# Threshold attention and a Fourier mixer: bit operations of the weight conversion moved to PSUM, tau's transfer and the first transpose rearranged

## The chip, the cores and the metric

The kernel runs on one core of one Trainium2 chip, in one launch. The metric is the device time in microseconds (us). The core has a matrix engine (PE), a vector engine (DVE), a scalar engine (ACT), a general engine (POOL) and SP, which here only issues transfers. Each engine works through its own queue in program order, and engines wait for each other by semaphores. SBUF is the large on-chip memory, PSUM the small one into which PE writes.

## The reference

Inputs q, k, v are float32 of shape (8, 8, 576, 64); the two weight matrices, 512x2048 and 2048x512, come as float64.

```python
scores = scale * np.matmul(q, k.transpose(0, 1, 3, 2))
thresh = np.max(scores, axis=-1, keepdims=True) - tau
scores = np.where(scores >= thresh, scores, -1000000000.0)
attn = np.exp(scores - np.max(scores, axis=-1, keepdims=True))
attn = attn / (np.sum(attn, axis=-1, keepdims=True) + 1e-09)
x = np.matmul(attn, v)              # heads side by side: (8, 576, 512)
u = x + np.real(np.fft.fft(np.fft.fft(x, axis=1), axis=2))
un = (u - mean(u)) / np.sqrt(var(u) + 1e-06)
out = u + np.maximum(un @ w_ch1, 0.0) @ w_ch2
```

## The kernel before

**Attention.** Two heads make a pair, four pairs a batch. A pair is worked in five steps t = 0 to 4 of 128 query rows for each head (the fifth holds the two ends of 64). A step is: `scores` (PE, tile sc, L431 and L437), the row maximum `neg` (DVE, L455), the exponential `e` (ACT, L463) with the threshold `thr` (L467), the comparison with the threshold, which also sums the row (DVE, L471), and the reciprocal of the sum `den` (L485). One step later PE transposes e into the tiles pe and pw (`transposed_weights`, L534 to L552), ACT copies these into SBUF (ends and e_t, L540 to L556), and PE multiplies with v in the tile pv (`weighted_values`, L581); DVE or ACT takes the product out as x (L589). `prep_pair` transposes k and q of the next pair on DVE (kT, L402 and L403; qT, L405), `scale_q` multiplies q beforehand (L389 on ACT for the first pair, L391 on POOL for others), and `load_pair`, `load_v` issue the transfers, on SP's queue but for the first pair's k, which goes through ACT's.

**Conversion of the weights.** Each float64 weight matrix is read as pairs of 32-bit words in 16 chunks of 128x512 and rebuilt as float32. `convert` is a generator whose stages the steps call one by one: transfer of the raw words; then two bit operations on DVE, one cutting out the upper fraction bits (L297), one the exponent (L300); then on ACT fraction to float (L305) and exponent to a power of two (L308); then on DVE the lower word added (L312); then on POOL the product with the power (L317); at last the sign on ACT (L319) and its product on POOL (L320). Before the change the bits are written into the destination in SBUF, and the exponent into a spare region of SBUF, `power`, which ACT overwrites with the power of two.

One chunk of w_ch1 goes with each of the first 16 steps of batch 0 (`step`); the 16 of w_ch2 go with the steps of batch 1 by the table PLAN (`second_batch`), in which three steps, 5, 8 and 9, hold two chunks. POOL and DVE also take the column means out of w_ch1 (L377), with PE's help (pm, pr).

**Other work.** From batch 1 on, PE also does the Fourier mixing (py, pa) and the channel layers of the batch before (`channels` and `channels_in_quarters`: ph L814 and L918, po L840 and L1082, transposed rows pn L774), handed out between the steps by a budget. Where nothing else is due in batch 0, `busy` fills PE with matmuls on ones (pd, L112).

**Order and buffers.** In batches 0 and 1 the order of each engine is written out by hand: it is the order of the code. The kernel uses eight banks of PSUM: the two sc tiles hold two each, and all other tiles in PSUM (pd, pe, pw, pv, pm, pr, py, pa, pn, ph, po) share the pool with the tag "mm" of four banks. A tile of this pool starts when the last reader of the bank's former tile is done. Transfers wait by eight semaphores used in turn, so a transfer can wait for the one eight places before it.

Of the kernel before, what the change touches and what calls it, by code (L numbers as in the profile page):

```python
# [10 lines left out]
INT32 = mybir.dt.int32  # L11
UINT32 = mybir.dt.uint32
ALU = mybir.AluOpType
ACT = mybir.ActivationFunctionType
# [33 lines left out]
def kernel(  # L48
# [12 lines left out]
    nc = tc.nc  # L61
    B, H, S, D = q.shape
# [11 lines left out]
    WC = 512  # L74
# [10 lines left out]
    ps = ctx.enter_context(tc.tile_pool(name="ps", bufs=2, space=bass.MemoryType.PSUM))  # L85
# [38 lines left out]
    def load_pair(n, queue=nc.sync):  # L124
        b, p = n // NPAIR, PAIRS[n % NPAIR]
        hs = [2 * p + (j + p) % 2 for j in range(2)]


        raws = []
        for src, name, eng in ((q, "q_in", nc.sync), (k, "k_in", queue)):  # L130
            raw = sb.tile([128, S], FP32, tag=name, bufs=1, name=name)
            for j, h in enumerate(hs):
                for g in range(2):
                    p = 64 * j + 32 * g
                    eng.dma_start(
                        out=raw[p : p + 32, :].rearrange("p (r d) -> p r d", d=32),
                        in_=src[b, h, :, 32 * g : 32 * g + 32].rearrange(
                            "(r p) d -> p r d", p=32
                        ),
                    )  # L140
            raws.append(raw)
        loaded[n] = raws
# [10 lines left out]
            nc.sync.dma_start(out=vt[64 * j : 64 * j + 64, 8 + j, :], in_=v[b, h, 512:576, :])  # L153

    tau_t = const.tile([128, 1], FP32, name="tau_t")
    nc.scalar.dma_start(out=tau_t[:, :], in_=tau.partition_broadcast(128))
    load_pair(0, nc.scalar)


    ident = const.tile([128, 128], FP32, name="ident")  # L160
# [5 lines left out]
    for u in range(2):  # L166
# [14 lines left out]
        out=q_scale[:], in0=tau_t[:], scalar1=0.0, scalar2=SCALE, op0=ALU.is_ge, op1=ALU.mult  # L181
# [3 lines left out]
        out=below[:], in0=tau_t[:], scalar1=0.0, scalar2=-3.0e38, op0=ALU.is_lt, op1=ALU.mult  # L185
# [3 lines left out]
        out=tau_pos[:], in0=tau_t[:], scalar1=0.0, scalar2=-1.0, op0=ALU.max, op1=ALU.mult  # L189
# [87 lines left out]
    shift = const.tile([128, 1], FP32, name="shift")  # L277
    nc.vector.memset(shift[:], -float((1023 - 127) << 23))

    def convert(src, dst, raw, power):  # L280

        if src.dtype == FP32:
            nc.sync.dma_start(out=dst, in_=src)
            return
        nc.sync.dma_start(out=raw, in_=src.bitcast(INT32).rearrange("p (c n) -> p c n", c=2))
        pairs = raw.rearrange("p c (n two) -> p c n two", two=2)
        low, high = pairs[:, :, :, 0], pairs[:, :, :, 1]
        dst = dst.rearrange("p (c n) -> p c n", c=2)  # L290
        bits = dst.bitcast(INT32)
        power = power.rearrange("p (c n) -> p c n", c=2)
        sign = high.bitcast(FP32)

        yield

        nc.vector.tensor_scalar(  # L297
            out=bits, in0=high, scalar1=0xFFFFF, scalar2=None, op0=ALU.bitwise_and
        )
        nc.vector.tensor_scalar(  # L300
            out=power, in0=high, scalar1=20, scalar2=0x7FF,
            op0=ALU.logical_shift_right, op1=ALU.bitwise_and,
        )
        yield
        nc.scalar.activation(out=dst, in_=bits, func=ACT.Copy, bias=1.0, scale=2.0**-20)  # L305


        nc.scalar.activation(  # L308
            out=power, in_=power, func=ACT.Relu, bias=shift[:, :], scale=float(1 << 23)
        )  # L310
        yield
        nc.vector.scalar_tensor_tensor(  # L312
            out=dst, in0=low.bitcast(UINT32), scalar=2.0**-52, in1=dst,
            op0=ALU.mult, op1=ALU.add,
        )
        yield
        nc.gpsimd.tensor_tensor(out=dst, in0=dst, in1=power.bitcast(FP32), op=ALU.mult)  # L317
        yield
        nc.scalar.activation(out=sign, in_=high, func=ACT.Sign)  # L319
        nc.gpsimd.tensor_tensor(out=dst, in0=dst, in1=sign, op=ALU.mult)  # L320
# [74 lines left out]
    def prep_pair(n):  # L395

        q_raw, k_raw = loaded.pop(n)  # L400
        kT = sb.tile([128, D + S], FP32, tag="kT", name="kT")
        nc.vector.transpose(kT[:, D : D + S], k_raw[:, :])  # L402
        nc.vector.transpose(kT[64:128, 0:D], k_raw[64:128, 512:S])  # L403
        qT = sb.tile([128, S], FP32, tag="qT", bufs=1, name="qT")
        nc.vector.transpose(qT[:, :], q_raw[:, :])  # L405
        heads[n] = (qT, kT, v_in[n % 2])
        if n + 1 < B * NPAIR:
            load_pair(n + 1)
# [95 lines left out]
    def transposed_weights(i):  # L504
        for _ in weights_in_parts(i):
            pass
# [670 lines left out]
    def step(i):  # L1177

        n, t = divmod(i, NT)
        scores(i)  # L1180

        def stages(count):
            for _ in range(count if i - 1 in chunks else 0):
                next(chunks[i - 1], None)

        def next_stages():
            stages(2)

        def last_stage():
            stages(1)  # L1190
            chunks.pop(i - 1, None)

        if t == 1 and n > 0:
            softmax(i, lambda: weighted_values(n - 1, 1), next_stages, last_stage)
            load_v(n + 1)
        elif t == 3:
            softmax(i, lambda: weighted_values(n, 0), next_stages, last_stage)
        else:
            softmax(i, None, next_stages, last_stage)
        if t == 1 and n > 0:  # L1200
            pass
        elif later and later[0][0] <= i:
            later.pop(0)[1](i)
        else:
            busy(2 if i < NCHUNK else 1)
        if t == 2:
            scale_q(n + 1)
        if t == 3:
            prep_pair(n + 1)
        if t == 1:  # L1210
            prep_ends(n)
        if i in chunks:
            next(chunks[i])
        if i > 0:
            transposed_weights(i - 1)
        if i in chunks:
            next(chunks[i])
        while after and after[0][0] <= i:
            after.pop(0)[1]()
        if i > 0 and i + 3 < NCHUNK:  # L1220
            chunks[i + 3] = w1_chunk(i + 3)
        if t == 2 and n > 0:
            folds.append(fold_rows(n - 1))
        if folds and next(folds[0], True):
            folds.pop(0)
# [26 lines left out]
    chunks = {0: w1_chunk(0)}  # L1252
# [27 lines left out]
    chunks = {}  # L1280

    def advance(at):
        for run in chunks.get(at, ()):
            next(run, None)

    def transfers(first):
# [32 lines left out]
    def second_batch(i):  # L1319

        nonlocal budget
        n, t = divmod(i, NT)
        first = i - per_batch
        if first != 1:
            scores(i)
        if first == 0:

            transposed_weights(i - 1)
        softmax(
            i, None, lambda: (advance(first - 1), advance(first - 1)), lambda: advance(first - 1)  # L1330
        )
        chunks.pop(first - 1, None)
        transfers(first)
        fold_more()
        if first == 0:
            weighted_values(n - 1, 1)
            scores(i + 1)
            column_means(LAST)
            copy_mean(LAST)
            folds.append(fold_rows(n - 1))  # L1340
            while folds:
                fold_more()
            load_v(n + 1)
            start_batch(0)
            mix(3)
            mix(3)
        elif first == 1:
            mix(3)
            transposed_weights(i - 1)
            mix(2)  # L1350
            mirrored(LAST)
            for c, eng in ((1, nc.vector), (3, nc.vector), (0, nc.gpsimd), (2, nc.gpsimd)):
                less_mean(eng, LAST, c)
            advance(first)
            advance(first)
        elif first == 2:
            mix(2)
            transposed_weights(i - 1)
            mix(2)
            weighted_values(n, 0)  # L1360
            advance(first)
            advance(first)
        else:
            fill()
            transposed_weights(i - 1)
            advance(first)
            advance(first)
            fill()
            if t == 3:
                prep_pair(n + 1)  # L1370
            fill()
            if t == 2:
                weighted_values(n, 0)
            if t == 0:
                weighted_values(n - 1, 1)
                folds.append(fold_rows(n - 1))
                load_v(n + 1)
        if t == 1:
            prep_ends(n)
        if t == 2:  # L1380
            scale_q(n + 1)
        if first == 16:
            fold_halves(1)
        if first < 3:
            budget += 3 * per_slot
# [10 lines left out]
    for i in range(2 * per_batch, total + 1):  # L1396
# [4 lines left out]
        n, t = divmod(i, NT)  # L1401
# [79 lines left out]
```

## Time and profile before

| | |
|---|---|
| three timed runs | 1632.99, 1632.99, 1630.95 us |
| the profiled execution | 1633.26 us, span 1631.3 us, PE clock 0.994 of full speed |
| PE busy | 1583.8 us (97%) |
| weight loads into PE (PEld) | 1248.7 us (77%) |
| DVE busy | 1173.4 us (72%) |
| ACT busy | 817.8 us (50%) |
| POOL busy | 659.3 us (40%) |

Busy shares are means over stages that have different limits; a stage is read from the table of busy time by stretches. The chain of work that ended last is followed back from the end, and tells at each step what released it. In a line such as `w<-hs` the tile before the arrow is written, the one after it read, with buffer numbers left out; "x16" counts instructions, and a note in brackets says how long the engine was idle before it and for whom it waited. A line with DMA in it is a transfer, one with a q after the engine (SPq, ACTq) the issue of one.

### The profile page before, as it was taken

The page shows a single profiled execution, that of the slowest core. Times are in us where ns is not written, and L with a number is a line of the kernel's source. Part 1 is how long each engine was busy: PE and PEld are TensorE (multiplying, and loading weights), DVE is VectorE, ACT ScalarE, POOL GpSimd, SP SyncE. Part 2 cuts the span into 40 slices and gives each one's busy share as a digit, 9 for nine tenths or more (in the row PEclk, how much of TensorE's full clock was granted, in tenths as well). Part 3 has the DMA queues.
Part 4 walks back from the last instruction along what each step waited for, and adds up shares of the span by engine and source line. Part 5 has one row for each costly group of instructions (what it writes and reads, how often), then busy time and mean ns, then how long its engine had stood idle before and what let it go on. Part 6 is the DMA issues. An engine that isn't in the chain of part 4 may idle for free.

```text
span 1631.3 us, 27898 instructions
## 1 busy us (share of the span) xinstructions
PE 1583.8 (97%) x10346; PEld 1248.7 (77%) x10346; DVE 1173.4 (72%) x2518; ACT 817.8 (50%) x1738; POOL 659.3 (40%) x875
## 2 busy tenths in 40 slices
PE   8998999999999999999999999999999999999998
PEld 4555655577887888878888778877878788889998
DVE  7997886667758686857576868786787869664445
ACT  5765665544455454645445546454636455523111
POOL 6784673042421452244342244224352344124332
PEclk9999999999999999999999999999999999999999
DMA  6423222101110101110011010111111110000000
GB/s 162 123 56 113 74 75 57 40 17 22 20 38 17 34 9 43 23 29 16 21 23 36 17 34 11 41 23 35 17 27 32 22 29 2 14 7 7 14 14 14
DMA packets 203084, 57.41 MB, mean 35 GB/s; under 512 B 193827, under 2 KB 193829, under 8 KB 202950
## 3 DMA queue, kind: packets, MB, share of 16 engines
q1 hardware_dynamic: 200438, 55.34, 14.5%
q8 instruction: 82, 1.34, 0.4%
q10 hardware_dynamic: 2512, 0.30, 0.1%
q14 instruction: 52, 0.43, 0.1%
HBM read 46.02 MB, written 9.44 MB: 34 GB/s over the span
## 4 chain that ended last, share of the span: by engine, by line
PE 77%; DVE 14%; ACT 4%; POOL 2%; issue 2%; DMA 1%; SPq 1%; DVEq 0%; ACTq 0%; POOLq 0%
PE ph L918 24%; PE po L1082 20%; PE pv L581 9%; PE sc L431 7%; PE pw L552 6%; PE po L840 3%; DVE neg L455 2%; DVE e L471 2%; PE ph L814 2%; PE sc L437 1%; ACT e L463 1%; PE pn L774 1%; PE py L684 1%; PE pa L701 1%; DVE hs L1043 1%
## 5 line engine op out<-in xcount | busy, mean ns | idle before, releaser
L463 ACT ACTIVATE e<-sc,neg 128x576 f32<-128x576 f32 x288 | 212.5, 738 | 224.7 <-DVE neg L455 224.5
L455 DVE TENSOR_REDUCE neg<-sc 128x1 f32<-128x576 f32 x288 | 207.3, 748 | 161.6 <-PE sc L431 149.7
L471 DVE SCALAR_TENSOR_TENSOR e<-sc,thr,e 128x576 f32<-128x576 f32 x288 | 229.4, 812 | 42.2 <-ACT thr L467 40.4
L1082 PE MATMUL po<-w,hs 128*128 128x256 f32 x1024 | 246.2, 383 | 0.0
L1082 PEld LDWEIGHTS po<-w,hs 128*128 128x128 f32 x1024 | 186.1, 190 | 33.8 <-issue 12.8
L918 PE MATMUL ph<-u_t,w 128*128 128x128 f32 x1536 | 188.1, 277 | 0.0
L431 PE MATMUL sc<-kT,qT 64*128 64x288 f32 x1024 | 174.4, 433 | 12.6 <-DVE e L471 11.1
L918 PEld LDWEIGHTS ph<-u_t,w 128*128 128x128 f32 x1536 | 180.2, 193 | 5.0 <-issue 3.7
L552 PE MATMUL pw<-ident,e 128*128 128x128 f32 x1152 | 170.7, 275 | 7.8 <-ACT y_o L689 2.3
L554 ACT COPY e_t<-pw 128x512 f32<-128x512 f32 x256 | 148.8, 594 | 48.9 <-PE pw L552 48.2
L927 DVE TENSOR_TENSOR hs<-ph,hs 128x512 f32<-128x512 f32 x160 | 106.9, 685 | 70.7 <-PE ph L918 54.0
L431 PEld LDWEIGHTS sc<-kT,qT 64*128 64x128 f32 x1024 | 96.0, 187 | 78.1 <-issue 37.5
L552 PEld LDWEIGHTS pw<-ident,e 128*128 128x128 f32 x1152 | 134.9, 141 | 27.2 <-ACT y_o L689 4.2
L918 PE MATMUL ph<-t_u,s_w 128*128 128x128 f32 x1024 | 126.7, 277 | 2.1 <-POOL t_u L892 1.8
L918 PEld LDWEIGHTS ph<-t_u,s_w 128*128 128x128 f32 x1024 | 119.9, 192 | 7.4 <-issue 4.6
L1082 PE MATMUL po<-hs,s_tile 128*128 128x256 f32 x512 | 121.5, 381 | 0.0
L796 DVE SCALAR_TENSOR_TENSOR u<-po,rstd,u 128x256 f32<-128x256 f32 (+1 forms) x164 | 75.3, 483 | 63.9 <-PE po L1082 62.8
L492 ACT ACTIVATE e<-e,den 128x576 f32<-128x576 f32 x96 | 74.6, 777 | 76.5 <-DVE den L485 76.0
L1082 PEld LDWEIGHTS po<-hs,s_tile 128*128 128x128 f32 x512 | 94.0, 190 | 13.7 <-issue 2.5
L935 ACT ACTIVATE hs<-hs 128x512 f32<-128x512 f32 x112 | 69.2, 630 | 61.6 <-DVE hs L927 61.6
L614 POOL TENSOR_TENSOR half<-x 128x287 f32<-128x287 f32 x48 | 40.5, 865 | 119.5 <-ACT x L587 61.1
L1078 POOL TENSOR_TENSOR hs<-hs,s_tile 128x512 f32<-128x512 f32 x32 | 42.0, 1314 | 107.9 <-PE po L1082 85.0
(194 smaller groups left out, 2899.5 us busy)
## 6 DMA issues: line engine op xcount, KB each, us to landing
hs<-in_moe_w_ch_dram SPq DMA_DIRECT2D x23, 512.0 KB, 4.8
q_in<-in_q_dram SPq DMA_DIRECT2D x128, 72.0 KB, 2.5
out_dram<-u SPq DMA_DIRECT2D x36, 256.0 KB, 2.2
k_in<-in_k_dram SPq DMA_DIRECT2D x124, 72.0 KB, 2.5
v_in<-in_v_dram SPq DMA_DIRECT2D x64, 128.0 KB, 2.4
w<-in_moe_w_ch_dram SPq DMA_DIRECT2D x6, 512.0 KB, 3.6
stage<-in_moe_w_ch_dram SPq DMA_DIRECT2D x3, 512.0 KB, 3.6
v_in<-in_v_dram SPq DMA_DIRECT2D x64, 16.0 KB, 2.2
```

Of the source, the lines that this page charges most:

```text
L431: nc.tensor.matmul(sc[j][:, c, 0:HALF], qT[hp, 128 * t : 128 * t + 128], kT[hp, k0 + HALF * c : k0 + HALF * (c + 1)], start=True, stop=True,)
L455: nc.vector.tensor_reduce(out=neg[:, j : j + 1], in_=sc[j][:, :, 0:HALF], axis=AXIS_XY, op=ALU.max, negate=True,)
L463: nc.scalar.activation(out=ej, in_=sc[j][:, :, 0:HALF], func=ACT.Exp, bias=neg[:, j : j + 1], scale=1.0)
L471: nc.vector.scalar_tensor_tensor(out=ej, in0=sc[j][:, :, 0:HALF], scalar=thr[:, j : j + 1], in1=ej, op0=ALU.is_ge, op1=ALU.mult, accum_out ...
L492: nc.scalar.activation(out=e[:, S : 2 * S], in_=e[:, S : 2 * S], func=ACT.Copy, scale=den[:, 1:2])
L552: nc.tensor.transpose(pw[:, c, :], e[:, c0 : c0 + 128], ident[:, :])
L554: nc.scalar.copy(e_t[:, 4 * j : 4 * j + 4, qs], pw[:, :, :])
L581: nc.tensor.matmul(pv[64 * j : 64 * j + 64, 0:m], vt[:, 2 * c + j, :], e_t[:, 4 * j + c, 0:m] if c < 4 else ends[:, 0, 0:m], start=(c == 0 ...
L796: nc.vector.scalar_tensor_tensor(out=u, in0=product, scalar=self.rstd[:, t : t + 1], in1=u, op0=ALU.mult, op1=ALU.add,)
L918: nc.tensor.matmul(banks[name][:, 128 * q : 128 * q + 128], left[c][:, 512 * part + 128 * q : 512 * part + 128 * q + 128], right[c], start ...
L927: nc.vector.tensor_tensor(out=to, in0=bank, in1=to if other is None else other, op=ALU.add)
L1082: nc.tensor.matmul(bank[:, 0 : DM // 2], left[p], right[p], start=start and p == 0, stop=p == NK - 1, skip_group_check=True,)
```

## The change

The bits and the exponent go into two new PSUM tiles of the "mm" pool, and ACT reads them there; `power` receives only the power of two. Both stages (bit operations and ACT's reading) of a chunk now stand together, after the transposes of the step, in all three places that call them. At the start, tau's transfer (128 copies of one number) is issued behind the first pair's k on ACT's queue, and the transpose of the first pair's q is cut in two, 128 and 448 columns.

```diff
     tau_t = const.tile([128, 1], FP32, name="tau_t")
+    load_pair(0, nc.scalar)
     nc.scalar.dma_start(out=tau_t[:, :], in_=tau.partition_broadcast(128))
-    load_pair(0, nc.scalar)
...
-        bits = dst.bitcast(INT32)
         power = power.rearrange("p (c n) -> p c n", c=2)
...
+        bits, exponent = (
+            ps.tile([128, 2, WC // 2], INT32, tag="mm", bufs=4, name=name)[:, :, :]
+            for name in ("bits", "exponent")
+        )
         nc.vector.tensor_scalar(
             out=bits, in0=high, scalar1=0xFFFFF, scalar2=None, op0=ALU.bitwise_and
         )
         nc.vector.tensor_scalar(
-            out=power, in0=high, scalar1=20, scalar2=0x7FF,
+            out=exponent, in0=high, scalar1=20, scalar2=0x7FF,
             op0=ALU.logical_shift_right, op1=ALU.bitwise_and,
         )
...
         nc.scalar.activation(
-            out=power, in_=power, func=ACT.Relu, bias=shift[:, :], scale=float(1 << 23)
+            out=power, in_=exponent, func=ACT.Relu, bias=shift[:, :], scale=float(1 << 23)
         )
...
-        nc.vector.transpose(qT[:, :], q_raw[:, :])
+
+        for c0, c1 in ((0, 128), (128, S)) if n == 0 else ((0, S),):
+            nc.vector.transpose(qT[:, c0:c1], q_raw[:, c0:c1])
...
-        if i in chunks:
-            next(chunks[i])
         if i > 0:
             transposed_weights(i - 1)
         if i in chunks:
+            next(chunks[i])
             next(chunks[i])
...
+    def first_stages(at):
+        for run in chunks.get(at, ()):
+            next(run, None)
+            next(run, None)
...
             transposed_weights(i - 1)
-            advance(first)
-            advance(first)
+            first_stages(first)
             fill()
```

The last part stands in the three branches of `second_batch`. In the changed kernel the lines move by up to seven: the bit operations are L301 and L304, ACT's reading L309 and L312, the lower word L316.

More of the change, by code (lines that the diff above doesn't have):

```diff
@@ L1360, in second_batch @@
             weighted_values(n, 0)
-            advance(first)
-            advance(first)
+            first_stages(first)
         else:
@@ L1365, in second_batch @@
             transposed_weights(i - 1)
-            advance(first)
-            advance(first)
+            first_stages(first)
             fill()
```

## Prediction

> **What bounds the kernel now.** I read the table of stages first (busy time of each engine between given times), then the chain of work that ended last, then the timelines of single engines around the changed instructions. Batches 0 and 1 run to about 130 and 300 us; only there are weights converted, 16 chunks in each. The table's columns are the stretch and its length, the busy time and instructions of PE, PEld (weight loads), DVE, ACT and POOL, PE's clock, the DMA share and GB/s:
>
> ```profile
> 26.60:43.70 17.10, 15.00 (x76) 8.60 (x74) 16.29 (x35) 12.93 (x27) 10.85 (x11) 1.00 0.69 188
> 43.70:56.70 13.00, 12.96 (x72) 7.52 (x74) 12.62 (x30) 10.07 (x21) 9.66 (x14) 1.00 0.27 67
> 56.70:110.00 53.30, 49.31 (x245) 27.49 (x245) 51.17 (x107) 39.54 (x80) 45.09 (x50) 0.97 0.38 98
> 161.50:255.00 93.50, 85.83 (x408) 52.87 (x408) 80.59 (x170) 65.37 (x137) 60.37 (x68) 0.95 0.31 77
> ```
>
> DVE works 51.17 of 53.30 us from 56.7 to 110 and 16.29 of 17.10 before 43.7: it is the bound there. From 43.7 to 56.7 PE has no gap, and in batch 1 (161.5 to 255) PE (92%) and DVE (86%) take turns. After 300 us nothing is converted. So the change can act on the first 255 us alone; what it wins or loses there shifts all the rest.
>
> How long the two bit operations (L297, L300) take depends on POOL. The timeline, POOL and DVE together:
>
> ```profile
> 19.43 1.28 POOL L317 TENSOR_TENSOR w<-w,hs 128x512 f32<-128x512 f32 x1
> ...
> 19.77 1.22 DVE L297 TENSOR_SCALAR w<-hs 128x512 int32<-128x512 int32 x1
> ...
> 20.79 1.36 POOL L320 TENSOR_TENSOR w<-w,hs 128x512 f32<-128x512 f32 x1
> ...
> 20.91 1.51 DVE L300 TENSOR_SCALAR hs<-hs 128x512 int32<-128x512 int32 x1
> ...
> 34.52 0.38 DVE L297 TENSOR_SCALAR w<-hs 128x512 int32<-128x512 int32 x1
> ```
>
> The pair at 34.52 is undisturbed: its L300 starts at 34.83, 0.31 us later. L297 at 19.77 ends 0.28 us after POOL's L317 (20.71), L300 0.27 us after L320 (22.15): each waits for POOL's instruction to end and then runs its own 0.3 us. From the start of L297 to the end of L300 the 16 pairs of batch 0 take 25.3 us in all, those of batch 1 27.3 us: 1.6 and 1.7 us a pair where 0.7 would do.
>
> Two more places matter. The chain of waits says what releases chunk 2, the third one, and what a pair of 512-wide operations with a PSUM operand costs:
>
> ```profile
> 22.24 4.33 DMA hs<-in_moe_w_ch_dram
> 26.59 1.48 DVE w L297
> ...
> 64.33 1.20 DVE w L377 x2
> ```
>
> At 26.59 DVE waits for chunk 2's transfer, not for its own earlier work. And in the first step of batch 1 with two chunks PE runs ahead of DVE (timelines of PE and DVE):
>
> ```profile
> 174.92 0.60 PE L774 MATMUL pn<-ident,u_t 128*128 128x128 f32 x4
> 175.36 2.80 PE L814 MATMUL ph<-u_t,w 128*128 128x384 f32 x8
> 178.34 2.37 PE L581 MATMUL pv<-e_t,v_rev 128*64 128x320 f32 x16 [0.19 <-ACT e_t L556]
> ...
> 178.22 1.11 DVE L297 TENSOR_SCALAR w<-w 128x512 int32<-128x512 int32 x1
> ...
> 184.09 0.75 DVE L455 TENSOR_REDUCE neg<-sc 128x1 f32<-128x576 f32 x1
> ```
>
> [...] L377 (PSUM and SBUF in) takes 673 to 693 ns in all 8 cases and L471 784 to 820 ns in all 288, with POOL busy or not. A DVE output in PSUM is in no row of it. [...] A bits tile of 512 int32 is one bank; the scores hold four, so the four "mm" banks are all that PE has for everything else.
>
> **The change, part by part.** The built order shows the same instructions in the same order on every engine, but for tau's transfer, the split transpose and one pair of v_rev copies on POOL. So only durations and waits differ.
>
> *The bit operations' price.* Nearest rows: L377, 512 wide with one PSUM operand, 1.20 us for two in the chain, so 0.60[...]. I take 0.60 each, 1.20 a pair. Below: 0.55[...]; above: 0.67, as for each of the two maxima (L455, 1.33 for two). [...]
>
> *Batch 0.* Summed over all pairs DVE saves 25.3 - 16 x 1.28 = 4.8 us (an end is recorded 0.08 after the next start), but only pairs on the chain count. Chunks 0 and 1 save 1.1 us in all, yet DVE then waits longer for the transfer that lands at 26.57: nothing. From there, each pair's slot in the chain against 1.20: 26.59 -0.71, 34.6 +0.2, 38.25 -0.56; 43.9 to 56.7 is PE's, 0; 63.1 -0.03, 68.4 -0.56, 74.1 -0.44 (only L297 is on it), 80.4 +0.45, 85.1 -0.29, 94.5 +0.2, 98.3 -0.90, 104.6 -1.09. Sum -3.7 us. POOL works without a gap from 90.4 to 108.3, then idles 1.88 us for DVE; this lets the last two savings (2.0) through, just.
>
> *Batch 1.* At 157.3 the pair delays POOL, which is on the chain there: L723 and L727 (rows of one partition) take 0.87 and 1.07 us instead of 0.68, and near 148.6 L727 0.99 instead of 0.69: -0.9. The four operations at 203.7 take 2.83 of the chain against 2.4: -0.4. At 229.4 the chain leaves L297 for ACT: -0.2 after PE's own 0.30 us of slack. The pairs at 172, 189 and 212 end earlier, but then DVE waits for PE's scores: 0.
>
> *New waits.* PE's next tile must wait until ACT (L305, L308) has read the bank. In batch 0 that is the previous step's chunk, read long before; the one that bites, the filler matmul at 63.07 (read done at about 64.3), delays only filler, and PE had 2 us in that step. In batch 1 the tile pn takes the bank of the bits that DVE writes at 178.22: 0.60, then ACT's L305 0.63, so about 179.5 instead of 174.92: PE stands 4.6 us. Behind it in PE's queue are ph (2.8), pv (2.9) and the next scores (1.2), which end at 187.0 instead of 182.4. DVE's maximum of these scores, at 184.09 before, starts 2.9 us later; it had waited for others until then, so 1.7 us of the stall is absorbed, and about 0.2 more in the next pipeline step: +2.7. Later cases, by the same reading: ph at 203.92 waits to 204.95, but PE then had 0.62 and 1.92 us idle: 0; pw at 250.76 waits 0.7 us, before a wait of 1.00 on ACT: 0. DVE's own new waits: the exponent waits for ACT's copy of a transposed tile (L540 or L554), with the next maximum queued behind. By the times of before that copy is done in all but one pair of batch 0 (at 55.6, 0.1 us); at 162.85 the bits wait 0.85 us for a relu on ACT, ahead of an idle DVE: 0.
>
> *ACT* reads from PSUM: L554, 512 wide from PSUM, 594 ns, L305 from SBUF 631: 0.04 less each, hidden behind DVE.
>
> *Start.* k's four issues start at 0.71 instead of 1.16, and the fourth, which waited for tau until 3.6, goes at about 2.2; tau then waits for k's first landing (about 4.0) and lands 2.9 to 4.2 us later, at 6.9 to 8.2. DVE's four tau operations (0.5) stand ahead of the transposes of k. q is scaled at 7.0 to 8.3 and the first part transposed 0.25 later: first scores at 8.9 to 10.0 instead of 9.77. ACT queues scale_q behind it, PE the scores. All of it ends before chunk 2's transfer, and SP's queue, which sets that, keeps its order and its first wait (the k transfer issued at 1.16): 0, bounds -0.3 and +0.3.
>
> Sum: -3.7 - 0.9 - 0.4 - 0.2 + 2.7 = -2.5 us; some of the chain's savings run into the next path a little behind, so I take -2.2 us, on the profile's span 1631.3. The three timed runs lie between 1630.95 and 1632.99, this execution took 1633.26. I forecast 1630.8. About 0.2% (3.3 us) is what a measurement of this kernel can tell from no change.
>
> **The rivals.** *Faster: [...].* If PE's stall is hidden (DVE reaches the chunk earlier, or ACT reads at once), the sum is -5.2, 1627.8; if DVE bounded batch 1 as it does batch 0, all of the 11.6 us of DVE time (52.6 - 32 x 1.28) would be the ceiling, 1621.4. For: DVE at 95%. Against: DVE idle 14% in batch 1. *Slower: PE is held by its banks.* Three steps of batch 1 convert two chunks, four banks each, so all that PE has. If PE is held in each as at 174.9, 3 x 4.6 = 13.8 us less 5.2 gives +8.6, 1641.6; it decides once unabsorbed stalls exceed 5.2 us, and shows from 8.5. For: the built order has PE's tile wait for the conversion's bank in all three. Against: at 203.9 and 213.2 PE was not ahead of DVE. *It does not do what it says:* if a PSUM output still waits for POOL, the gains vanish and the stall stays: +2.7, 1635.7.
>
> **How the numbers follow.** Forecast 0.45 (1628 to 1633, which holds the price's bounds of 0.55 and 0.67: -1.0 and +1.4 over the 10 pairs of batch 0's chain); faster rival 0.37; banks 0.12[...]. So faster 0.37, same 0.48, slower 0.15. The range, 1626.0 to 1636.5, takes in most of the faster rival and the milder cases of the stall; the likeliest case's own is 1628 to 1633.
>
> **What would show it.** L301 and L304 at 0.6 to 0.7 us with a spread under 0.1; chunk 2 still waiting for its transfer near 26.5, with over 1 us idle on DVE; the maxima near 110 about 3.5 us earlier; pn in the first two-chunk step waiting some 4 us for ACT. I am wrong if the bit operations still spread to 1.5 us, if chunk 2's transfer comes earlier, or if PE waits for L309 or L312 in many steps.

## The result, and the profile after

The changed kernel takes 1651.87 us (median of four, 1648.68 to 1655.40) beside 1632.59 us for the kernel before in the same session (four, 1630.95 to 1632.99): the ratio is 1.0121, interval 1.0094 to 1.0147. It is 19.3 us slower. The forecast was 1630.8 us, range 1626.0 to 1636.5; the time lies outside it, on the side that had 15% of the chance.

The table of stages of the changed kernel, same columns, two of the stretches that were shown of before:

```profile
56.70:110.00 53.30, 48.73 (x245) 27.46 (x242) 51.05 (x111) 39.17 (x80) 42.74 (x51) 0.97 0.38 95
161.50:255.00 93.50, 72.72 (x342) 43.29 (x342) 60.58 (x133) 50.83 (x107) 48.10 (x61) 0.91 0.25 65
```

Batch 0 looks as it did. In batch 1 PE works 72.7 of 93.5 us instead of 85.8, and DVE 60.6 instead of 80.6: every engine waits more, in a stretch for which the prediction's terms come to only +2.1 us (2.7 - 0.4 - 0.2). The bit operations themselves are what they were to be. Rows of the two lines (engine, operation, count, then shortest, median and longest duration in ns):

```profile
L301 DVE TENSOR_SCALAR bits<-hs x23: 666/684/696, 15.0 to 236.4; 128x512 int32<-128x512 int32 x23
L304 DVE TENSOR_SCALAR exponent<-hs x23: 670/684/694, 15.6 to 237.0; 128x512 int32<-128x512 int32 x23
```

They no longer wait for POOL, and the time is lost elsewhere. Who PE waited for between 160 and 300 us (total us, times, longest), first in the kernel before, then in the changed one:

```profile
PE sc L431 <- DVE e L471: 3.3, 4, 1.9
PE ph L814 <- POOL u_t L727: 2.0, 1, 2.0
```

```profile
PE ph L820 <- ACT e_t L560: 16.2, 6, 5.1
PE pn L780 <- ACT w L309: 4.6, 1, 4.6
PE ph L820 <- ACT ends L550: 1.8, 1, 1.8
PE ph L820 <- ACT w L309: 1.7, 2, 0.9
```

The second row is the stall that the prediction had found. The first one is new: ph, the product of the tokens with w1 in a filler, waits for L560, ACT's copy of the transposed weights pw to e_t. ph reads no e_t. So it must be waiting for the bank that this copy reads from; the experiments test that. PE's timeline of the changed kernel shows the first long wait for a copy, and after it the wait of pn:

```profile
165.77 0.38 PE L558 MATMUL pw<-ident,e 128*128 128x128 f32 x2
168.76 4.28 PE L820 MATMUL ph<-u_t,w 128*128 128x384 f32 x8 [2.61 <-ACT e_t L560]
...
174.41 0.60 PE L558 MATMUL pw<-ident,e 128*128 128x128 f32 x4
179.59 1.11 PE L780 MATMUL pn<-ident,u_t 128*128 128x128 f32 x4 [4.57 <-ACT w L309]
180.50 5.15 PE L820 MATMUL ph<-u_t,w 128*128 128x384 f32 x8
```

In the kernel before the same ph followed pw without a gap, and ACT copied pw only later:

```profile
169.41 1.04 PE L552 MATMUL pw<-ident,e 128*128 128x128 f32 x8
170.29 2.75 PE L814 MATMUL ph<-u_t,w 128*128 128x384 f32 x8
...
172.42 1.08 ACT L554 COPY e_t<-pw 128x512 f32<-128x512 f32 x2
```

Why the copy comes so late is in ACT's timeline of the changed kernel at that place:

```profile
165.89 0.74 ACT L469 ACTIVATE e<-sc,neg 128x576 f32<-128x576 f32 x1 [3.13 <-DVE neg L461]
...
167.85 0.37 ACT L546 COPY ends<-pe 128x256 f32<-128x256 f32 x1
168.12 1.08 ACT L560 COPY e_t<-pw 128x512 f32<-128x512 f32 x2
```

ACT idles 3.13 us for DVE's maximum, then runs this step's exponential, and only then the copies of pe and pw, which belong to the step before. That is the order in which `second_batch` calls things: softmax first, `transposed_weights(i - 1)` after it. In the kernel before the next ph on PE did not need those banks, so ACT could be late: ph had been running for 2.1 us when the copy of pw began. Now ph does need one, and behind ph stand the next scores; without them DVE has no maximum, and without the maximum ACT has no exponential. The run ahead of PE, which had hidden this loop, is gone.

The banks explain why. The four mm banks go round in the order in which tiles are asked for. Before, a step asks for pe, pw, pw and then ph: ph gets the bank of the tile ahead of pe. Now it asks for pe, pw, pw, bits, exponent, ph: ph gets the first pw's, and the wait in the trace is for the copy of a pw.

How far ahead or behind the steps of each kernel start (ACT's thr of a step, against the step of the kernel before; us, worked out from one trace each; kernels that are alike in batch 0 differ there by up to 1.9 us, so that only the larger steps speak). The last seven columns belong to experiments below:

| step at | changed | order only | batch 0 | batch 1 | banks only | one bank | two-chunk | one-chunk |
|---|---|---|---|---|---|---|---|---|
| 12.49 | +0.18 | +0.24 | +0.28 | +0.31 | +0.11 | +0.12 | +0.30 | -0.20 |
| 109.46 | -2.09 | +0.07 | -1.48 | +1.33 | -0.54 | -1.54 | -2.09 | -2.32 |
| 141.02 | -1.82 | +0.07 | -1.52 | +1.34 | -0.53 | -1.59 | -1.65 | -1.69 |
| 170.83 | -4.30 | +0.07 | -2.46 | -1.12 | -1.50 | -4.19 | -3.33 | -4.17 |
| 185.58 | +5.60 | +0.07 | -2.68 | +6.25 | +4.26 | -0.75 | +0.83 | +0.39 |
| 217.46 | +5.16 | +0.09 | -2.69 | +7.34 | +6.54 | -0.63 | -1.58 | +2.85 |
| 252.38 | +20.88 | +0.02 | -2.89 | +21.14 | +22.24 | +9.79 | -0.10 | +18.47 |
| 293.67 | +20.88 | +0.02 | -2.91 | +21.13 | +22.24 | +10.14 | -0.12 | +18.46 |

The changed kernel is 4.3 us ahead at 170.8 and 20.9 behind at 252.4; from there to the last step compared nothing changes. 25.2 us are lost in some 80 us.

### The profile page after: what moved, and what is told of

It reads as the page before. It is cut to its first block, busy times and chain, and to the rows that moved or that the text cites. A ratio compares the mean times of both kernels' runs of the same rounds, so it can differ in the third digit from the quotient of the medians.

```text
span 1652.2 us, 27935 instructions
## 1 busy us (share of the span) xinstructions
PE 1586.9 (96%) x10346; PEld 1248.4 (76%) x10346; DVE 1164.0 (70%) x2519; ACT 816.9 (49%) x1738; POOL 651.0 (39%) x875
## 3 DMA queue, kind: packets, MB, share of 16 engines
q8 instruction: 82, 1.34, 0.4%
## 4 chain that ended last, share of the span: by engine, by line
PE 77%; DVE 14%; ACT 5%; issue 2%; POOL 1%; DMA 0%; DVEq 0%; ACTq 0%; POOLq 0%
PE ph L924 23%; PE po L1088 19%; PE pv L587 9%; PE sc L437 8%; PE pw L558 5%; PE ph L820 3%; PE po L846 3%; DVE neg L461 3%; DVE e L477 2%; ACT e L469 2%; PE sc L443 1%; DVE hs L1049 1%; PE pn L780 1%; PE py L690 1%; PE pa L707 1%
## 5 line engine op out<-in xcount | busy, mean ns | idle before, releaser
L437 PE MATMUL sc<-kT,qT 64*128 64x288 f32 x1024 | 170.7, 431 | 8.3 <-DVE e L477 6.7
L560 ACT COPY e_t<-pw 128x512 f32<-128x512 f32 x256 | 148.6, 593 | 49.3 <-PE pw L558 48.6
L820 PE MATMUL ph<-u_t,w 128*128 128x384 f32 (+1 forms) x256 | 70.8, 429 | 20.6 <-ACT e_t L560 16.2
```

Of the source, the lines that this page charges most:

```text
L437: nc.tensor.matmul(sc[j][:, c, 0:HALF], qT[hp, 128 * t : 128 * t + 128], kT[hp, k0 + HALF * c : k0 + HALF * (c + 1)], start=True, stop=True,)
L560: nc.scalar.copy(e_t[:, 4 * j : 4 * j + 4, qs], pw[:, :, :])
L820: nc.tensor.matmul(ph[:, a:z], w1[c][:, 128 * j : 128 * (j + 1)], u_t[:, c, at : at + z - a], start=(c == 0), stop=(c == ND - 1), skip_gro ...
```

## The experiments

All are made from the changed kernel. In most of them `convert` has one more argument that says whether a chunk's bit operations write to PSUM; otherwise they write to w1 or w2 and the spare room, as before:

```diff
-    def convert(src, dst, raw, power):
+    def convert(src, dst, raw, power, psum):
...
+        bits, exponent = dst.bitcast(INT32), power
+        if psum:
+            bits, exponent = (
-        bits, exponent = (
```

Line numbers are two or three higher in most of these kernels. Every ratio below is to the kernel before, measured beside it, whose medians were 1632.1 to 1632.9 us.

### Which part of the change costs

The first kernel keeps the new start and the new order of calls, with no chunk in PSUM (`psum` is False everywhere).

> Change as it is, but both bit operations write to SBUF again in both batches; what is left is tau's transfer behind the first pair's, the split transpose of q and the two stages called together. Theory (in batch 1 the conversion's tiles take the PSUM banks that PE's tiles had, so that ph waits for ACT's copies of the same step): nothing is taken here, so within 0.6 us of before, 1632.6. Rival (the new start or the new order of the calls moves DVE's and ACT's work and costs PE its run ahead): most of the loss stays, 1645 to 1652.

Measured: 1631.22 us, ratio 0.9993 (0.9985 to 1.0001), a little under the theory's 1632.6 but not clear of no change. The rival falls: start and order cost nothing. In the trace this kernel runs within 0.1 us of the kernel before from 29.9 us to the end of the table above.

PSUM for the w1 chunks of batch 0 alone (`w1_chunk` passes True, `second_chunk` False):

> PSUM for the bit operations of batch 0 alone; batch 1 converts in SBUF as before. Theory of the banks: the gain of batch 0 stays (steps of batch 0's end started 1.8 us earlier in the changed kernel's trace) and all stalls of PE for ACT's copies between 160 and 275 us go: 1630.8, 1629.5 to 1631.5. Rival (writes to PSUM by DVE themselves slow PE or ACT wherever they fall): about half of the loss stays, some 1642.

Measured: 1630.00 us, ratio 0.9985 (0.9979 to 0.9992). As the theory has it: batch 0's gain alone, and PE's waits from 160 to 300 us are again about those of before, with this row on top and no ph or pn for a copy or for the conversion:

```profile
PE sc L439 <- DVE e L479: 3.3, 4, 1.9
```

And for batch 1 alone:

> PSUM for the bit operations of batch 1 alone; batch 0 converts in SBUF as before. Theory of the banks: the whole loss and none of batch 0's gain: 1651.9 + 1.8 = 1653.7, 1650 to 1657. Rival (writes to PSUM slow the kernel wherever they fall): some 1642.

Measured: 1651.38 us, ratio 1.0126 (1.0108 to 1.0145): the whole loss, a little below the 1653.7 of the theory and far from the rival's 1642. Its wait table has the same two rows on top:

```profile
PE ph L822 <- ACT e_t L562: 16.2, 6, 5.1
PE pn L782 <- ACT w L311: 4.6, 1, 4.6
```

The fourth keeps PSUM for batch 0 and the first two chunks of batch 1 (`second_chunk` passes `j >= 14`):

> PSUM for batch 0 and the first two chunks of batch 1, of whose tiles no ph of a filler came to stand in the way; the other 14 chunks of batch 1 in SBUF. Theory of the banks: the changed kernel stood 4.3 us ahead at 166 us, before the first long stall; kept, that gives 1628.3, 1627.5 to 1630.5. Rival (any PSUM tile of batch 1 costs PE its run ahead, the gain at 166 us is given back at once): slower than the kernel with batch 0 alone, 1631 to 1634.

Measured: 1629.24 us, ratio 0.9980 (0.9973 to 0.9986). In the theory's range, and 3.6 us faster than the kernel before by the medians, 22.6 faster than the changed one; its interval overlaps that of the kernel with batch 0 alone, so that the two chunks add anything is not shown.

### Is it the banks, or the writing and reading?

Here all bit operations stay in SBUF, but each conversion of batch 1 asks for two banks at the same place; DVE writes one column of each, and nothing reads them. The two memsets a chunk are extra work that the reference does not need; by the 59 ns of a memset of one column in the kernel before (L278) I estimate them at 0.06 us each, 1.9 us in all 32.

```diff
-        bits, exponent = (
-            ps.tile([128, 2, WC // 2], INT32, tag="mm", bufs=4, name=name)[:, :, :]
-            for name in ("bits", "exponent")
-        )
+        bits, exponent = dst.bitcast(INT32), power
+        for name in ("bits", "exponent") if psum else ():
+            unread = ps.tile([128, 2, WC // 2], INT32, tag="mm", bufs=4, name=name)
+            nc.vector.memset(unread[:, 0, 0:1], 0)
```

> Bit operations in SBUF everywhere, as in the kernel that keeps only the new order; but each conversion of batch 1 takes the same two banks as in the changed kernel: DVE writes one column of each (a memset, about 0.06 us), and nobody reads them, so that PE's later tiles move on by two banks and the bank is free as soon as DVE has written. Theory (the move of PE's tiles by two banks makes ph wait for ACT's copies): nearly the whole loss without batch 1's gain, and pn's stall 0.6 us shorter: 1652, 1645 to 1657. Rival (the banks are held too long by ACT's late reads of bits and exponent): no reads, so little loss, 1632 to 1638. Second rival (DVE's long writes to PSUM hinder PE or ACT): no long writes, 1631 to 1633.

Measured: 1656.94 us, ratio 1.0152 (1.0138 to 1.0166). The whole loss is there, without a long write to PSUM and without a read by ACT of these banks. Both rivals fall. PE's waits from 160 to 300 us in this kernel:

```profile
PE ph L820 <- ACT e_t L560: 8.2, 3, 3.1
PE ph L820 <- ACT ends L546: 7.3, 2, 4.6
PE ph L820 <- ACT ends L550: 3.7, 1, 3.7
PE pn L780 <- DVE exponent L300: 3.5, 1, 3.5
```

ph waits 19.2 us in all for ACT's copies of pw and pe (8.2 + 7.3 + 3.7); pn's 3.5 us are for the memset (L300; the unread tile has the exponent's name).

With the bits alone in PSUM in batch 1 PE's tiles move on by one bank:

```diff
+            bits = ps.tile([128, 2, WC // 2], INT32, tag="mm", bufs=4, name="bits")[:, :, :]
+        if psum == 2:
+            exponent = ps.tile(
+                [128, 2, WC // 2], INT32, tag="mm", bufs=4, name="exponent"
+            )[:, :, :]
```

> As the changed kernel, but in batch 1 only the bits go to PSUM, the exponent to SBUF as before (no room taken by it). Theory: PE's tiles move on by one bank instead of two; ph then waits for ACT's copy of pe (ends), which stands just ahead of that of pw on ACT: each stall of ph is only about 0.5 us shorter, 1648, 1643 to 1651. Rival (two banks at once are too many, one can be spared): the loss goes, 1630 to 1635.

Measured: 1643.23 us, ratio 1.0073 (1.0061 to 1.0086), at the edge of the theory's range and well above the rival's. Where ph now waits is as foreseen: for the copy of pe (ends, the line just ahead of that of pw on ACT).

```profile
PE ph L823 <- ACT ends L549: 13.4, 5, 4.6
PE pn L783 <- ACT ends L553: 2.6, 1, 2.6
```

So the move of the tiles decides which copy is awaited. The loss is a little over half and not nearly all of it: pn waits 2.6 instead of 4.6 us, and by the table this kernel is still ahead at 217 us, where the changed kernel is 5.2 behind. I had underestimated that.

### Is it the order?

Now the conversion asks for its two banks after the second filler instead of before it, in steps 3 on of batch 1:

```diff
             transposed_weights(i - 1)
-            first_stages(first)
             fill()
+            first_stages(first)
```

> As the changed kernel with both banks in both batches, but in steps 3 on of batch 1 the conversion's first stages are called after the second filler instead of before it, so that this filler's ph and pn come next after pw in the order of banks, as in the kernel before, and the conversion's tiles after them. Theory: the stalls of that filler on ACT's copies go, those of the third filler and of the next step (one pw or pe on bits or exponent) stay or come new: 1634, 1629 to 1642. Rival (the loss comes from PSUM being full, wherever the tiles stand in the order): 1648 to 1654.

Measured: 1636.33 us, ratio 1.0027 (1.0016 to 1.0037). With as many tiles in the same four banks, three quarters of the loss are gone (1.0121 to 1.0027). The waits of ph for the copies of pw fall from 16.2 to 5.4 us, and a new one of pv for L311, ACT's read of the bits, takes 3.5:

```profile
PE ph L822 <- ACT e_t L562: 5.4, 3, 2.5
PE pv L589 <- ACT w L311: 3.5, 1, 3.5
```

The last test of the mechanism moves ACT's copies: in steps 3 on of batch 1 `transposed_weights(i - 1)` is called ahead of the softmax.

```diff
-        if first == 0:
+        if first == 0 or first > 2:
             transposed_weights(i - 1)
         softmax(
...
             fill()
-            transposed_weights(i - 1)
             first_stages(first)
```

It was made twice, first with PSUM for batch 0 and two chunks alone:

> The kernel with PSUM for batch 0 and two chunks of batch 1, and in steps 3 on of batch 1 the transposes of the step before's weights are called ahead of the softmax, right behind the scores, instead of after the first filler: ACT then copies pe and pw before this step's exponentials. The measure for the next kernel, and by itself open: ACT's copies (1.4 us a step) now stand ahead of the exponentials, but fall into the time of DVE's maxima (1.3 us): 1629 to 1634, against 1629.2 without the move.

Measured: 1638.08 us, ratio 1.0036 (1.0024 to 1.0049), slower than I had expected: PE's transposes come so early that they wait 7.0 us for POOL's rec and its scores 3.9 us for DVE. Then with PSUM for all chunks:

> The changed kernel (PSUM for all chunks of both batches) with the same move of the transposes. Theory (ph waits because ACT's copy of pw stands behind exponentials that wait for DVE's maximum of the same step): ph hardly waits for the copies of pw any more, 16.2 us before; what is left above the kernel with two chunks is about the 4.9 us of the two-chunk steps: 1636, 1631 to 1641. Rival (two fewer banks are too few in whatever order ACT works): 1647 to 1655.

Measured: 1637.46 us, ratio 1.0034 (1.0021 to 1.0046). With the copies called early, PSUM for the other 14 chunks costs nothing that can be measured (1.0034 against 1.0036); with the copies called late, the same 14 chunks cost 22.6 us (1651.87 against 1629.24). PE's waits from 160 to 300 us:

```profile
PE pn L782 <- ACT w L311: 5.3, 1, 5.3
PE pe L545 <- POOL rec L505: 3.5, 3, 1.6
PE pe L542 <- ACT w L311: 2.7, 2, 1.9
PE ph L822 <- ACT e_t L562: 1.5, 5, 0.5
```

The wait of ph for the copies is down from 16.2 to 1.5 us. The stall of pn is still there, 5.3 us, and pe waits 2.7 us for ACT's read of the bits, both partly in place of the waits for rec (3.5 instead of 7.0). So some of the 14 chunks' cost may only have moved into waits that this order makes anyway; the fall of ph's wait for the copies is the cleaner evidence. As a measure the early copies do not pay: with PSUM for batch 0 and two chunks they make the kernel slower, 1.0036 against 0.9980.

### Which steps

PSUM in batch 1 for the six chunks of the two-chunk steps alone (j 11, 10, 7, 6, 5 and 4):

> As the changed kernel, but in batch 1 only the six chunks of the three steps that convert two at once use PSUM; the other ten convert in SBUF. Theory (steps with one chunk stall as well, where ph follows the pair): only the step around 180 us and its kin cost here, 4.6 us of pn and what the two later ones give: 1636, 1632 to 1640. Rival (the slower rival of the prediction, PE held in the two-chunk steps alone): the whole loss, 1648 to 1654.

Measured: 1634.14 us, ratio 1.0013 (1.0006 to 1.0019): 4.1 us more than with batch 0 alone. PE is held there once, at pn, and briefly twice more:

```profile
PE pn L782 <- ACT w L311: 4.5, 1, 4.5
...
PE ph L822 <- ACT w L311: 1.8, 2, 1.0
```

The complement, PSUM for the ten chunks that are alone in their step:

> The complement of the kernel with the two-chunk steps: PSUM for batch 0 and for the ten chunks of batch 1 that are converted one in a step; the six of the two-chunk steps in SBUF. If the losses add up: 1651.5 - 4.9 = 1646.6, 1644 to 1650, with ph's waits for the copies of pw nearly all there and none of pn. If the steps hang together (a stall in one makes or spares one in the next): away from this by over 4 us, down to 1638 or up to 1652.

Measured: 1652.75 us, ratio 1.0122 (1.0107 to 1.0138): the whole loss. The losses do not add up, so that of the two cases expected it is the second: the steps hang together. This kernel has two waits of nearly 4 us for a copy (of pw and of ends) that the changed kernel does not have or has shorter, while the wait of pn is not there:

```profile
PE ph L822 <- ACT e_t L562: 17.0, 6, 5.1
PE ph L822 <- ACT ends L552: 3.7, 1, 3.7
```

And PSUM for batch 0, the first two chunks of batch 1 and the first two-chunk step alone (`j >= 14 or j in (11, 10)`), for the size of the prediction's one stall:

> The kernel with PSUM for batch 0 and two chunks of batch 1, and besides PSUM for the two chunks of the first two-chunk step alone, where pn waits 4.6 us for ACT's read of the bits. The prediction's term for this stall, 2.9 of 4.6 us unabsorbed less 0.2: 1629.2 + 2.7 = 1631.9, 1631 to 1633. If nothing of the stall is absorbed: 1633.8. If it is absorbed wholly by later waits: 1629.2.

Measured: 1634.92 us, ratio 1.0012 (1.0003 to 1.0020), against 0.9980 without that step: 0.32%, or 5.2 us (2.8 to 7.7 by the ends of the two intervals). The traces say the same: between the steps at 170.8 and 185.6 us this kernel loses 5.7 us on the kernel before, the one without that step gains 0.2. That is more than the whole wait of 4.42 us, and the reason is in PE's timeline of this kernel:

```profile
175.64 1.12 PE L782 MATMUL pn<-ident,u_t 128*128 128x128 f32 x4 [4.42 <-ACT w L311]
176.54 5.29 PE L822 MATMUL ph<-u_t,w 128*128 128x384 f32 x8
```

pn takes 1.12 us instead of 0.60, ph 5.29 instead of 2.80: after the wait PE is slow. The table of stages of the changed kernel, in short stretches around the same place, has the granted clock in the third column from the end:

```profile
175.00:179.50 4.50, 0.01 (x1) 0.00 (x0) 4.39 (x12) 3.69 (x8) 3.02 (x4) 0.89 0.00 0
179.50:180.50 1.00, 0.91 (x5) 0.92 (x6) 1.00 (x2) 1.00 (x3) 0.11 (x1) 0.50 0.58 74
180.50:182.00 1.50, 1.50 (x4) 0.88 (x4) 0.18 (x1) 1.50 (x6) 0.00 (x0) 0.50 0.80 295
```

PE has just stood for 4.5 us and then runs at half clock, 0.50. In finer stretches the half clock begins at 178.5 us, still in the wait, and ends at 185.3.

## Why the prediction was wrong, point by point

**The bit operations' price: right.** 666 to 699 ns recorded, 0.59 to 0.69 in the chain, where I took 0.60 with bounds of 0.55 (an estimate that no row of before showed) and 0.67, and no wait for POOL. Of the 64 instances of L301 and L304, 50 ran with POOL busy for over nine tenths of their time, in 667 to 696 ns, and seven with POOL idle, in 666 to 699; in the kernel before, with the output in SBUF, L297 and L300 took 384 to 1522. That an output in PSUM would not wait for POOL had been an assumption: the rows of before showed PSUM as input only. One sum of before was read a little low: the 16 pairs of batch 1 take 27.6 us and not 27.3; that moves only the ceiling of the faster rival.

**Batch 0, -3.7 us: the right sign, two to three times too large.** At 109.5 us the changed kernel is 2.1 us ahead, the one with batch 0 alone 1.5; by the runs, batch 0 is worth 0.9993 - 0.9985, 0.08% or 1.3 us (the two intervals overlap; their ends allow at most 3.6). I had let the two last savings, 2.0 us together, through. But the waits for POOL were not gone; one came up at the next operation. The two engines at that place in the changed kernel:

```profile
99.17 1.49 POOL L649 TENSOR_TENSOR sums<-f 128x608 f32<-128x608 f32 x1
99.24 1.97 DVE L316 SCALAR_TENSOR_TENSOR w<-hs,w 128x512 f32<-128x512 uint32 x1
```

L316, the third DVE operation of a conversion, which reads and writes SBUF, comes earlier now and meets POOL's fold; it takes 1.97 us, and ends 0.55 after it. Before, the longest of its kind in batch 0 took 1.20. Its 16 instances in batch 0 sum to 13.0 us instead of 11.5. The kernel with batch 0 alone has the same meeting (2.00 us); that it accounts for the whole shortfall is not shown.

**POOL at 146 to 161, -0.9: about right.** The lead grows by 0.7 us between the steps at 141.0 and 160.3 (1.82 to 2.53), and by as much in the kernel with batch 1 alone (+1.34 to +0.63). The two smaller savings, -0.4 and -0.2, fall into the stretch of the stalls and can't be told apart there.

**Start, 0: right.** tau lands at 8.05 us and the first scores start at 9.94, both within what was foreseen; first thr 0.18 us later; the kernel with the new start and order alone is at 0.9993. DVE's own new waits, put at nothing, were right too: L301 waits once for a copy, 0.2 us, and L304 never.

**The stall of pn, +2.7: the mechanism and its place were right, the size was not.** The wait was read as 4.6 us and is 4.57. Absorbed 1.9, as I had said, would leave 2.7; the experiment gives 5.2. What the sum lacked is the half clock: 0.5 us on pn and 2.5 on ph (5.29 - 2.80). With them the estimate is 4.4 + 0.5 + 2.5 - 1.9 = 5.5, if 1.9 was absorbed as foreseen. The prediction had priced PE behind the wait as before it. The half clock here (0.50) lasted 6.8 us, from 178.5 to 185.3. It does not follow from a wait's length alone: after a wait of 2.61 us at 168.76 the clock was 0.50 as well (ph 4.28 us), while after 3.10 us at 194.00 ph took 2.85; the last section has more. In the changed kernel five groups of ph took 4.28 to 5.49 us instead of 2.85, 9.6 us more in all; in the kernel before, one did (4.79 at 213.22).

**"Later cases, by the same reading: ... 0": this is the step that failed.** It put at 0 what PE waited 18.0 us for: ph for ACT's copies of pw and pe (16.2 + 1.8). I had looked for tiles of PE that wait for the conversion's own banks, that is, for L309 and L312 (L305 and L308 of the kernel before). There are few: pn, and 1.7 us of ph. I had not asked what becomes of all the other tiles when two more are drawn from a ring of four: each later tile gets another bank, and so another reader to wait for. ph had been given a bank free long ago and was given one that ACT was about to read, in a program order in which ACT reads it after an exponential that waits for DVE. The kernel with the banks alone shows the whole loss with this and two short memsets a chunk, and in the kernels with the pair asked for later, or with ACT's copies called earlier, most of the loss is gone. The 24.3 us of such waits of PE (16.2 + 4.6 + 1.8 + 1.7) and the half clock make up more than the 25.2 us lost; that the rest fell into slack that PE had had is argued and not measured.

**The rivals.** The slower one had the right resource and sign (PE held by its banks) with the wrong place: it counted the three two-chunk steps, because all four banks are taken there. Those steps alone cost 4.1 us; the steps with one chunk, which take two banks of four, cost the whole. Not how many banks are taken, but whose bank comes next decided. The faster rival and "it does not do what it says", which had 0.06, half of it slower, fall.

**The signs.** Chunk 2 was to wait near 26.5 with over 1 us idle on DVE: it starts at 26.40 after 0.95, and the trace names PE's scores there, not the transfer; in the kernel with batch 0 alone it starts at 27.01 after 1.45, for the transfer. "I am wrong if PE waits for L309 or L312 in many steps" was itself a wrong sign: between 160 and 300 us PE waits for L309 three times only. (Before that it does so three times as well, 1.8 us in all, of which 1.2 are the filler matmul near 63 us that the prediction had foreseen.) The waits that cost the time are for copies that have nothing to do with the conversion.

**What stays open.** Why the loss with one bank is half and not most of it is described (pn's wait is shorter, the first stalls are fewer), but no run isolates it. The stalls of different steps do not add up, and how much slack took in between them I can only bound by the totals. The half clock makes it harder to tell, since it came after some of the waits and not after others (last section).

## What to carry to other kernels

When a change draws more tiles from a ring of buffers, work out whose buffer each later tile now gets, and when the reader of that buffer gets to it in its own engine's program; here the waits for the new tiles themselves were the small part (4.6 + 1.7 us beside 18.0). A copy that frees a buffer closes a loop when it stands behind work that waits for the engine which the buffer feeds. Moving the copies ahead opened this loop but cost 0.56% of its own; asking for the new tiles after the next tile of PE left 0.27% of loss; the two fastest kernels here (0.9985 and 0.9980) draw the extra tiles in batch 0 alone, or there and for two chunks more. And a wait of PE of some 2.5 to 5 us has to be priced with what follows it: in these traces between nothing (ph 2.85 us after 3.10) and 3.0 us more (pn and ph after 4.42).

## What the runs showed of the hardware

**The clock of PE.** In the changed kernel it was granted at 0.50 in five stretches between 160 and 300 us: 168.3 to 171.7, 178.5 to 185.3, 236.5 to 240.0, 246.8 to 250.2 and 263.8 to 270.7, so for 3.4 or 6.8 us each. Its trace has two more of 3.4 us (from 103.4 and 533.5 us), that of the kernel before three of 3.4 (from 104.5, 162.6 and 729.2) and one of 6.8 (from 210.3); the clock's record of each ends in one more. In the 3.4 us before those five stretches PE was busy for 1.25, 0.00, 0.85, 1.16 and 0.00 us. The length of a wait did not decide: the one of 3.10 us before 194.00 was followed by full clock, with PE busy for 2.15 and 1.58 us in the two stretches of 3.4 us that it falls into, and the shorter one of 2.52 us before 245.62 by half (the second column is PE's busy time, the third from the end the clock):

```profile
188.75:192.16 3.41, 2.15 (x18) 1.46 (x14) 2.75 (x5) 1.62 (x4) 0.30 (x1) 1.00 0.01 1
192.16:195.58 3.42, 1.58 (x5) 1.06 (x6) 3.28 (x10) 2.87 (x7) 3.42 (x3) 1.00 0.32 71
243.37:246.78 3.41, 1.16 (x4) 0.76 (x5) 3.31 (x10) 2.82 (x8) 2.62 (x3) 1.00 0.00 0
246.78:250.20 3.42, 3.42 (x8) 1.44 (x8) 0.51 (x2) 1.08 (x2) 3.42 (x8) 0.50 0.00 0
```

The eight matmul records of one ph took 4.28 to 5.49 us in or across the five stretches instead of 2.75 to 2.85. No run isolates what brings the half clock on, so what a wait will cost can't be told from its length by these runs. In batch 0 of the changed kernel PE waits 1.74 us for DVE before 102.09 us, and the clock is 0.50 from 103.4 to 106.8; its mean over the first 146 us is 0.99. In the kernel with PSUM for batch 0 and two chunks, whose program is the same up to there, that mean is 0.98. Between the steps at 109.5 and 114.4 us the first falls back by 0.3 us against the kernel before (-2.09 to -1.83), the second by 1.7 (-1.69 to +0.05); that execution, 1631.51 us, was the slowest of its 21. That the clock makes this difference, and how much of the spread between executions comes from it, was not measured.

**A bit operation into PSUM.** One of 512 int32 from SBUF to PSUM on DVE took 666 to 699 ns in all 64 instances of the changed kernel: 667 to 696 in the 50 with POOL busy for over nine tenths of the time, 666 to 699 in the seven with POOL idle.

**The wait that moved.** A wait for POOL that was taken away from one DVE operation came back in part on the next one that still works in SBUF (L316 at 99.24 us: 1.97 us, ending 0.55 after POOL's L649, instead of at most 1.20 in batch 0 of the kernel before).
